# A transformer block's list schedule: another table of times for the prologue, and other keys, engines and a DMA allowance for the end

## The chip, the cores and the metric

The kernel runs on one core of a Trainium2 chip. The metric is the device time of one execution in microseconds. TensorE (PE) does the matmuls, VectorE (DVE), ScalarE (ACT) and GpSimd (POOL) the elementwise work; SyncE (SP) issues nearly all DMAs of this kernel, in the order in which they stand in its queue. Each engine takes its instructions in program order and waits for what an instruction needs, so what stands behind a waiting instruction waits too.

## The reference

One block with 2048 positions, D = 512, 32 heads of 16, a causal window of 256 and a hidden width of F = 1792, all in fp32:

```python
mod = (silu(c) @ w_mod).reshape(1, 6, 1, 512)          # sa, ca, ga, sb, cb, gb
h = layernorm(x) * (1 + ca) + sa
q, k, v = split(h @ wqkv)                              # 32 heads of 16
p = softmax(where(0 <= i - j < 256, q @ k.T / 4, -1e9))
x = x + ga * ((p @ v) @ wo)
h = layernorm(x) * (1 + cb) + sb
x = x + gb * ((silu(h @ w1) * (h @ w3)) @ w2)
```

## The kernel before

Each fp32 operand is split into a high part, which an ACT copy rounds, and a low part, the difference, which DVE or POOL computes; each product is three matmuls (high by high, high by low, low by high), 128x128 by 128x512 for the most part. The FFN's products are taken over two-by-two blocks of positions and of weights with seven products instead of eight.

The work falls into three stages, and every instruction's place is fixed by a program that sorts before anything is emitted:

1. *The prologue*, about the first 98 us. It loads x, makes the modulation of c, normalises (LN1), transposes, splits the result into hT and computes the values, and with them the first three `unit_a` (a head group's q and k for 512 positions) and the first two `unit_b` (scores for the row maxima). Every step is recorded as `at(t, fn)` with a time out of the tables `W` (for all but the units) and `Y` (for the units here), and the steps are emitted sorted by that time.
2. *The units*, to about 450 us: 32 rounds with the times of table `X`.
3. *The end*: wo with the gated residual, LN2, the FFN. `Sched.deal` is a list scheduler. Every operation has an engine, a cost, the operations it needs and a key; the scheduler goes through time and gives each engine the ready operation with the smallest key. The last units are in it as `fixed`. Table `K` holds the offsets of the keys, and in `by` and `be` the engines of the multiplications and low parts of the attention's output (`by`) and of the later splits of the FFN's inputs (`be`). `PEM` is an allowance added between ACT, DVE or POOL and a PE operation that uses their result; `QUIET` and `TW` are two more constants of this plan's time. The scheduler's times serve the order only: on the chip the order stays, and the times are what they are.

Tiles and lines of the profile that the text speaks of:

- *Prologue.* L410 and L412 fill ringq and ringk (the buffers of q and k for the scores) with their constant rows on POOL; L330 is the reciprocal root of LN1 (`rs0r`, `rs1r`) on POOL, L335 and L336 its statistics and L340 its application to `xt` on DVE; L631 transposes on PE, L347 applies the modulation on ACT and writes `h`, L349 and L350 split it into hT on DVE (L349 is the CAST, the high part). L653 and L438 are the matmuls of the values and of q and k; L423 and L427 split the weights of q and k. L572, L578, L583 and L592 make a gate's row of the modulation, L593 stores it to `g_dr`; it shares the buffer `h` with L347. L451 is the low part of q and k (`qk`), L457 and L459 are the DMAs that bring it into ringk and ringq, L537 loads x, L545 the modulation's weights, L419 those of q and k. L485 are the scores on PE, L494 their row maxima on DVE; L503 and L509 turn the maxima over (`mr`).
- *Last units.* L753 are the scores again, L773 a mask on DVE, L766 and L768 the exponentials on ACT, L721 the products with the values.
- *Attention's output.* L1072 takes the reciprocals of the sums of the softmax, which go to a buffer in memory (`r_dr`); L1104 multiplies the output (loaded from `o_dr`) with them; L1096 and L1099 split the result (`o`, or `x1b` for one block) into high and low part; L1116 are the matmuls with wo.
- *LN2.* L985, L990 and L993 add the residual and take the statistics, L1004, L1007 (the root, on POOL) and L1010 the row factors, L1236 applies them, L1250 transposes, L1254 modulates, L1267 forms sums and differences of blocks, L1273 and L1275 split them into `b`.
- *FFN.* L967 and L968 split weights, high part and low part. L1378 are the up products, L1401 to L1421 the combination of the seven and the gating up to L1405, L1449 the split of its result, L1471 the down products, L1476 adds them to x. L877 is work on the weights of later passes (`e`, `jb`) that fills gaps of POOL.

Of the kernel before, what the change touches and what calls it, by code (L numbers as in the profile page):

```python
# [39 lines left out]
         10.575, 10.975, 11.087, 6.249, 6.261), o=(11.83, 12.324), job=(0.275, 3.004, 9.681), gate=7.93)  # L40
Y = dict(wqk=(0, 4, 5), pj=(0.0, 0.382, 0.764, 1.146, 1.528, 1.91, 2.292, 2.674, 3.056, 3.438, 3.82, 4.202),
         ev=(4.614, 4.813), mix=(5.0,), row=(4.9, 4.9, 4.9, 5.1, 5.1, 5.1, 6.4, 6.4, 6.4), mx=(0.0, 0.5, 1.0, 1.5,
         2.0, 2.5, 3.0, 3.5, 4.0, 4.5, 5.0, 5.5, 6.0, 6.5, 7.0, 7.5), tl=(0.402, 0.402, 0.402, 0.402, 0.402,
         0.402, 0.402, 0.402, 0.402, 0.402, 0.402, 0.402, 0.402, 0.402, 0.402, 0.402), mr=(8.402, 8.563,
         8.761, 9.49))
MODE = 'CDCPCDCP'
W = dict(m=0.15, s=0.1, a=0.29, t=0.541, p=0.377, vs=1.762, vo=0.422, wq=(-1.8, 1.47, 1.5), wv0=-1.811, wvh=(-0.7, -0.65, -0.6, -0.55), wvl=(-0.5, -0.31, -0.3, -0.25), wp=1, A0=2.1, h0=0.539, h=6, hb=6.874, ls=3.287, la=1.146, rf=(1.55, 1.56, 8.4), v=2, vt=1.75, mr=(-1.85, 1.55), mm=(2.6, 4.625, 5.85, 7.075), ml=(-1.79, 1.25, 2.0, 4.9), A=1.268, At=7.876, B=9.889)
MXB = 3
# [64 lines left out]
class Sched:  # L113
# [36 lines left out]
    def deal(self):  # L150
# [5 lines left out]
        banks, fixed = list(self.banks), list(self.fixed)  # L156
        held = dict.fromkeys(CAPS, 0)
        given = dict.fromkeys(CAPS, 0)
        order, self.dealt = [], []

        def push(o):
            insort(ready[o.eng], (o.key, o.seq, o))
# [5 lines left out]
        while left:  # L168
            best = None
            for e, lst in ready.items():  # L170
                t, pick = free[e], None
                for key, seq, o in lst:
                    s = o.est
                    new = [b for b in o.bank if b.i is None]
                    if new:
# [6 lines left out]
                        s = max(s, at)  # L182
                    if o.kb:
# [3 lines left out]
                        s = max([s] + [u + 0.01 for u in self.urgent if b <= u < end])  # L187
# [7 lines left out]
            if fixed and (best is None or fixed[0][0] <= best[0]):  # L195

                t, e = max(free[fixed[0][2]], fixed[0][0]), fixed[0][2]
# [7 lines left out]
            elif fixed and (best is None or fixed[0][0] <= best[0]):  # L205
                t, fn, e, occ = fixed.pop(0)
# [5 lines left out]
            s, o = best  # L212
# [11 lines left out]
            if o.kb:  # L224
                s = max(s, lanes.pop(0))
# [19 lines left out]
            for u in o.users:  # L245
                m = PEM if u.eng == "PE" and o.eng in ("ACT", "DVE", "POOL") else 0.0
                u.est = max(u.est, s + (o.lat + m if u.eng != o.eng or o.kb else o.occ))
                u.need -= 1
                if not u.need:
                    push(u)  # L250
# [7 lines left out]

QUIET = 1.5
KEY = 1.715  # L260
# [3 lines left out]
def us(t):  # L264
# [3 lines left out]

TW = (231.0, 241.0, 0.8, 0.65)

# [5 lines left out]
NPE = 3  # L276

PEM = 0.8

BY = ((("POOL", "POOL"),) * 3 + (("DVE", "DVE"),), (("POOL", "POOL"),) * 3 + (("DVE", "DVE"),),  # L280
      (("POOL", "DVE"),) * 3 + (("DVE", "DVE"),), (("POOL", "POOL"),) * 4)
K = dict(be=(('DVE', 'DVE'), ('DVE', 'POOL'), ('DVE', 'POOL'), ('POOL', 'POOL'), ('POOL', 'DVE'),
         ('POOL', 'DVE'), ('DVE', 'DVE')), hr=0.109, de=7.098, wo=-0.159, x1=5.764, xb=-29.382,
         xl=0.241, os=-0.129, ol=(-15.316, -4.484, -6.572, 4.956), pl=(3.999, 1.87, -4.828,
         102.62), pe=(0.982, -5.962, 56.258, 232.622), o=(1.381, 8.497, 20.124, -0.531), n=(1, 1,
         2, 1), w0=62.113, l2=0.424, f=1.543, fl=40.897, by=((('POOL', 'POOL'), ('DVE', 'DVE'),
         ('DVE', 'POOL'), ('DVE', 'DVE')), (('DVE', 'DVE'), ('DVE', 'POOL'), ('DVE', 'DVE'),
         ('DVE', 'POOL')), (('POOL', 'POOL'), ('POOL', 'DVE'), ('DVE', 'POOL'), ('POOL', 'DVE')),
         (('POOL', 'DVE'), ('DVE', 'POOL'), ('DVE', 'POOL'), ('DVE', 'POOL'))), w=0.559, dn=1.412,
         ds=0.003, l3=-0.027)  # L290
@with_exitstack
# [1314 lines left out]
```

## Time and profile before

| | |
|---|---|
| time, median of 3 runs | 959.67 us (958.03 to 962.35) |
| profiled execution | 961.9 us |
| its span | 960.2 us |
| PE busy | 918.5 us, 96% |
| DVE, ACT, POOL busy | 672.0, 524.0, 541.5 us |
| mean granted clock of PE | 0.984 |

A row of the timeline reads: start in us, length in us, engine, line, operation, output and inputs, and in brackets the idle time of that engine in front of it and what ended it. `[2.23 <-DMA ringq<-qk]` on a PE row says that PE had nothing to do for 2.23 us until that DMA landed. A row with xN is N instructions in one. A busy row of DVE or POOL can itself be longer than usual when both work at once. PEclk is the clock that PE was granted, 1.00 being full.

### The profile page before, as it was taken

The page shows a single profiled execution, that of the slowest core. Times are in us where ns is not written, and L with a number is a line of the kernel's source. Part 1 is how long each engine was busy: PE and PEld are TensorE (multiplying, and loading weights), DVE is VectorE, ACT ScalarE, POOL GpSimd, SP SyncE. Part 2 cuts the span into 40 slices and gives each one's busy share as a digit, 9 for nine tenths or more (in the row PEclk, how much of TensorE's full clock was granted, in tenths as well). Part 3 has the DMA queues.
Part 4 walks back from the last instruction along what each step waited for, and adds up shares of the span by engine and source line. Part 5 has one row for each costly group of instructions (what it writes and reads, how often), then busy time and mean ns, then how long its engine had stood idle before and what let it go on. Part 6 is the DMA issues. An engine that isn't in the chain of part 4 may idle for free.

```text
span 960.2 us, 16729 instructions
## 1 busy us (share of the span) xinstructions
PE 918.5 (96%) x5330; PEld 710.2 (74%) x5330; DVE 672.0 (70%) x1864; ACT 524.0 (55%) x1031; POOL 541.5 (56%) x691
## 2 busy tenths in 40 slices
PE   5999999999999999988986989999999999999998
PEld 2678677777777777755664878888888888888886
DVE  7576689898988989886568465765559645565455
ACT  3333677787867777766577653333446334433330
POOL 5211565666666576645565688977647456443420
PEclk9999999999999999999998999999999999999999
DMA  9531365555655655466870577754335413312102
GB/s 306 171 93 46 93 181 162 158 158 151 191 154 151 159 157 158 135 181 195 250 232 1 184 243 277 235 188 162 98 122 191 167 58 99 99 61 85 36 23 88
DMA packets 125020, 141.62 MB, mean 147 GB/s; under 512 B 60034, under 2 KB 72834, under 8 KB 124932
## 3 DMA queue, kind: packets, MB, share of 16 engines
q1 hardware_dynamic: 124212, 139.51, 47.7%
q10 hardware_dynamic: 720, 1.05, 0.4%
q8 instruction: 42, 0.69, 0.3%
q14 instruction: 46, 0.38, 0.1%
HBM read 85.72 MB, written 34.61 MB: 125 GB/s over the span
## 4 chain that ended last, share of the span: by engine, by line
PE 76%; DVE 8%; DMA 4%; POOL 3%; ACT 3%; issue 3%; SPq 2%; POOLq 0%; DVEq 0%; ACTq 0%
PE mx L1378 10%; PE st L1378 10%; PE pj L438 9%; PE st L753 8%; PE po L721 8%; PE mx L485 7%; PE mx L1471 7%; PE st L1471 6%; PE st L653 4%; PE pj L1378 3%; PE pj L1471 2%; POOL w L968 1%; POOL e L877 1%; PE mx L1116 1%; PE mx L572 1%
## 5 line engine op out<-in xcount | busy, mean ns | idle before, releaser
L494 DVE CUSTOM_DVE_ANT_0 junk<-mx,mskq 128x320 bf16<-128x320 f32 (+4 forms) x512 | 223.3, 464 | 36.1 <-PE mx L485 34.9
L968 POOL TENSOR_TENSOR w<-w,w 128x512 fp32r<-128x512 f32 (+2 forms) x56 | 107.4, 1931 | 117.1 <-ACT w L967 71.2
L485 PE MATMUL mx<-ringk,ringq 96*128 96x320 f32 (+4 forms) x512 | 154.5, 324 | 5.3 <-DVE mt L494 3.0
L753 PE MATMUL st<-ringq,ringk 98*128 98x256 f32 (+1 forms) x528 | 140.9, 335 | 7.1 <-DVE st L773 3.3
L780 POOL TENSOR_SCALAR_AFFINE_SELECT pt<-pt 128x256 f32<-128x256 f32 x224 | 91.4, 408 | 80.8 <-ACT pt L768 73.2
L438 PE MATMUL pj<-hT,wq 128*128 128x512 f32 x384 | 133.2, 405 | 1.6 <-DVE wq L427 0.8
L485 PEld LDWEIGHTS mx<-ringk,ringq 96*128 96x128 f32 x512 | 98.0, 192 | 45.3 <-DVE mt L494 24.7
L768 ACT ACTIVATE pt<-st 128x512 f32<-128x512 f32 (+1 forms) x198 | 115.4, 587 | 25.0 <-DVE st L773 9.3
L753 PEld LDWEIGHTS st<-ringq,ringk 98*128 98x128 f32 x528 | 90.9, 192 | 22.3 <-ACT pt L768 5.9
L721 PE MATMUL po<-pt,vS 128*17 128x384 f32 (+2 forms) x1408 | 93.1, 395 | 0.3 <-ACT pt L768 0.3
L438 PEld LDWEIGHTS pj<-hT,wq 128*128 128x128 f32 x384 | 68.5, 192 | 10.1 <-DVE wq L427 1.2
L1378 PE MATMUL mx<-b,w 128*128 128x512 f32 x270 | 67.7, 396 | 6.0 <-ACT t L1412 5.7
L1409 DVE TENSOR_TENSOR t<-mx,t 128x512 f32<-128x512 f32 x49 | 33.7, 688 | 45.6 <-PE mx L1378 26.0
L1378 PEld LDWEIGHTS mx<-b,w 128*128 128x128 f32 x270 | 51.2, 191 | 17.3 <-ACT t L1412 6.0
L1409 DVE TENSOR_TENSOR t<-st,t 128x512 f32<-128x512 f32 x47 | 32.4, 689 | 44.0 <-PE st L1378 22.8
L773 DVE COPY_PREDICATED st<-later,st 128x256 f32<-128x256 uint8 x112 | 47.4, 424 | 22.5 <-PE st L753 19.2
L721 PEld LDWEIGHTS po<-pt,vS 128*17 128x17 f32 x1408 | 34.8, 98 | 36.9 <-issue 19.0
L1449 ACT ACTIVATE wq<-g 128x512 fp32r<-128x512 f32 x28 | 17.7, 631 | 80.7 <-DVE g L1405 33.2
L761 DVE TENSOR_TENSOR st<-st,mskr 128x256 f32<-128x256 f32 x125 | 53.6, 429 | 8.8 <-PE st L753 8.8
L795 POOL TENSOR_SCALAR_AFFINE_SELECT sm<-sm 128x256 f32<-128x256 f32 x109 | 42.4, 406 | 28.3 <-ACT sm L785 27.2
L1378 PE MATMUL st<-b,w 128*128 128x512 f32 x234 | 57.9, 390 | 0.0
L451 POOL TENSOR_TENSOR qk<-qkr,qk 128x512 fp32r<-128x512 f32 x32 | 42.1, 1316 | 25.5 <-ACT qk L447 25.5
(262 smaller groups left out, 2009.5 us busy)
## 6 DMA issues: line engine op xcount, KB each, us to landing
ringk<-qk SPq DMA_DIRECT2D x96, 128.0 KB
ringq<-qk SPq DMA_DIRECT2D x192, 64.0 KB
o_dr<-os SPq DMA_DIRECT2D x32, 256.0 KB
w<-wsum SPq DMA_DIRECT2D x14, 512.0 KB
w<-w2g SPq DMA_DIRECT2D x14, 512.0 KB
jb<-in_w SPq DMA_DIRECT2D x24, 256.0 KB
wraw<-in_w SPq DMA_DIRECT2D x7, 768.0 KB
w<-wraw SPq DMA_DIRECT2D x14, 384.0 KB
```

What stands on the lines that cost most here:

```text
L438: nc.tensor.matmul(v["ps"], WQ[g][w][:, n // 3], hTp(i, n // 3, b * BT, BT), start=(n == 0), stop=(n == 3 * KC - 1))
L485: nc.tensor.matmul(v[i][:, :n], both_queries(a, gs), keys(NS, a, (gs + 1) * HP - n, n), start=True, stop=True)
L494: nc.vector.tensor_tensor_reduce(out=junk[:, :n], in0=v[i][:, :n], in1=mskq[:, WK - n:], scale=1.0, scalar=-3e38, op0=ALU.add, op1=ALU.max ...
L721: nc.tensor.matmul(po[32 * i:32 * i + DH + 1, qb * P:(qb + nq) * P], vS[:, kb, 4 * g + i], pts[i // 2][:, i % 2, c0:c0 + nq], start=first, ...
L753: nc.tensor.matmul(o, keys(NM, a, kb * P, P), queries(a, q, n), start=q == lo, stop=not plus and q + n == hi, skip_group_check=True)
L761: nc.vector.tensor_tensor(out=ps, in0=ps, in1=mskk[:, p:p + 1].to_broadcast([P, 2, P]), op=ALU.add)
L768: nc.scalar.activation(held[u, j, a][:, :, :n], v[j, a, 0].rearrange("p (h q) k -> p h q k", h=2)[:, :, :n], AF.Exp, scale=SCALE)
L780: nc.gpsimd.affine_select(out=pt[:, :, 2 * m], in_=pt[:, :, 0], **w)
L968: sch.op(eng, lambda: on_eng(eng).tensor_tensor(out=lo(), in0=src(), in1=hi().bitcast(F32), op=ALU.subtract), 0.06 + 0.0024 * n if eng == ...
L1378: nc.tensor.matmul(ps(bk), WT[s, n][w][:, col], BB[t, k][r], start=start and c == 0, stop=stop and c == 5, skip_group_check=True)
L1409: return nc.vector.tensor_add(o, x, y)
L1471: nc.tensor.matmul(ps(bk), tiles[hk + (h,)][:, i * P:(i + 1) * P], w2_of(last, y, f), start=(m == 0), stop=(m == 5))
```

## The change

Only numbers change, and one allowance is new. `Y` and `W` get other values, so the prologue's steps are sorted otherwise; `K` gets other keys and, in `by` and `be`, other engines; `QUIET`, `TW[3]` and `PEM` move. The new `DM` = 0.076 is added in the plan to the landing of a DMA that carries data for an operation of an engine other than SP, if the DMA starts before the last operation of the units that are in the plan as `fixed`. `X`, the table of the units, stays, and so do the operations of the end and their needs.

```diff
-W = dict(m=0.15, s=0.1, ..., rf=(1.55, 1.56, 8.4), ..., mm=(2.6, 4.625, 5.85, 7.075), ml=(-1.79, 1.25, 2.0, 4.9), A=1.268, At=7.876, B=9.889)
+W = dict(m=0.18, s=0.307, ..., rf=(-1.1, -0.393, 6.445), ..., mm=(3.653, 5.841, 7.356, 7.655), ml=(-1.346, 1.651, 2.536, 6.904), A=1.465, At=7.897, B=10.563)
...
+        late = lambda o, u, s, stop=fixed[-1][0]: o.kb and u.eng != "SP" and s < stop
...
             for u in o.users:
-                m = PEM if u.eng == "PE" and o.eng in ("ACT", "DVE", "POOL") else 0.0
+                m = PEM if u.eng == "PE" and o.eng in ("ACT", "DVE", "POOL") else DM if late(o, u, s) else 0.0
                 u.est = max(u.est, s + (o.lat + m if u.eng != o.eng or o.kb else o.occ))
...
-QUIET = 1.5
+QUIET = 1.487
...
-TW = (231.0, 241.0, 0.8, 0.65)
+TW = (231.0, 241.0, 0.8, 0.583)
...
-PEM = 0.8
+PEM = 0.998
+DM = 0.076
...
-K = dict(be=(('DVE', 'DVE'), ('DVE', 'POOL'), ('DVE', 'POOL'), ('POOL', 'POOL'), ('POOL', 'DVE'),
-         ('POOL', 'DVE'), ('DVE', 'DVE')), hr=0.109, de=7.098, wo=-0.159, x1=5.764, xb=-29.382,
+K = dict(be=(('POOL', 'DVE'), ('POOL', 'DVE'), ('DVE', 'POOL'), ('POOL', 'POOL'), ('POOL', 'POOL'),
+         ('POOL', 'POOL'), ('DVE', 'POOL')), hr=2.855, de=12.48, wo=-3.567, x1=16.6, xb=-38.041, xl=-26.167,
...
```

*The prologue, SP's queue ahead of the first scores.* `g_dr` is a gate's row, `ringk` and `ringq` the buffers of the scores, `xt` a tile of x, the `qk` tiles the high parts and (the last ringk and ringq here) the low part of the first unit. Before:

```order
L537 DMA xt<-in_x 128x512 x2
L593 DMA g_dr<-h_413 1x512
L457 DMA ringk<-qk_432 32x2x512
L459 DMA ringq<-qk_432 16x16x64 x2
L457 DMA ringk<-qk_432 32x2x512
L459 DMA ringq<-qk_432 16x16x64 x2
L593 DMA g_dr<-h_470 1x512
L537 DMA xt<-in_x 128x512 x2
L457 DMA ringk<-qk_452 32x2x512
L459 DMA ringq<-qk_452 16x16x64 x2
```

Now:

```order
L459 DMA ringq<-qk_432 16x16x64 x2
L457 DMA ringk<-qk_432 32x2x512
L459 DMA ringq<-qk_432 16x16x64 x2
L419 DMA wqr<-in_wqk 128x512
L537 DMA xt<-in_x 128x512 x2
L593 DMA g_dr<-h_486 1x512
L457 DMA ringk<-qk_432 32x2x512
L593 DMA g_dr<-h_498 1x512
L457 DMA ringk<-qk_453 32x2x512
L459 DMA ringq<-qk_453 16x16x64 x2
```

The two loads of x between the last gate row and the first unit's last rows now stand ahead of both gate rows, and so does the load of weights that followed.

*The prologue, POOL.* Before:

```order
L330 TENSOR_TENSOR rs1r<-rs1v,nhalf 128x4
L451 TENSOR_TENSOR qk_452<-qkr,qk_432 128x512
L665 MEMSET vS 128x384
L410 MEMSET ringq 98x1024 x2
L412 MEMSET ringk 2x2x512
```

Now:

```order
L330 TENSOR_TENSOR rs1r<-rs1v,nhalf 128x4
L410 MEMSET ringq 98x1024 x2
L412 MEMSET ringk 2x2x512
L451 TENSOR_TENSOR qk_453<-qkr,qk_432 128x512
L665 MEMSET vS 128x384
```

The last fills of the rings moved from behind the low part of the first unit to right behind the root of LN1's second block. On PE the first score now stands behind 66 matmuls of the values and 16 of q and k; it stood behind 55 and 14.

*The units' end, DVE.* L773 is the mask that PE waits for, L1104 and L1072 belong to the attention's output. Before:

```order
L773 COPY_PREDICATED st<-later,st 128x2x128
L1104 TENSOR_TENSOR wq_7426<-wq_7426,wq_7445 128x512
L1104 TENSOR_TENSOR qkr<-qkr,qk_7464 128x512
L1072 RECIPROCAL mT<-mT 32x128
L773 COPY_PREDICATED st<-later,st 128x2x128
L1099 TENSOR_TENSOR x1b<-qkr,x1b 128x512
L773 COPY_PREDICATED st<-later,st 128x2x128 x2
```

Now:

```order
L773 COPY_PREDICATED st<-later,st 128x2x128
L1104 TENSOR_TENSOR qk_7400<-qk_7400,qk_7413 128x512
L773 COPY_PREDICATED st<-later,st 128x2x128
L1104 TENSOR_TENSOR wq_7426<-wq_7426,wq_7447 128x512
L1072 RECIPROCAL mT<-mT 32x128
L1104 TENSOR_TENSOR qkr<-qkr,qk_7525 128x512
L773 COPY_PREDICATED st<-later,st 128x2x128 x2
```

One mask moved ahead of the multiplications and the reciprocal; the last two stand behind the multiplication of `qkr`, as before.

*The FFN's start, ACT.* L1412 copies the first product out of its bank (`mx` or `st`), L1273 are the high parts of `b`, L1096 those of the attention's last block. Before:

```order
L1254 ACTIVATE t_8172<-st,modc 128x512
L1273 ACTIVATE b_7816<-t_8157 128x512
L1273 ACTIVATE b_7800<-t_8172 128x512
L1096 ACTIVATE o_7150<-wq_8026 128x512
L1096 ACTIVATE o_7150<-qk_7899 128x512
L1273 ACTIVATE b_7808<-t_8149 128x512
L1273 ACTIVATE b_7812<-t_8187 128x512
L1412 ACTIVATE t_8196<-mx 128x512
```

Now:

```order
L1254 ACTIVATE t_8185<-mx,modc 128x512
L1273 ACTIVATE b_7789<-t_8168 128x512
L1273 ACTIVATE b_7781<-t_8160 128x512
L1273 ACTIVATE b_7773<-t_8185 128x512
L993 ACTIVATE st,sqB_8045<-x1b,nmB_8044 128x512
L1273 ACTIVATE b_7785<-t_8201 128x512
L1412 ACTIVATE t_8208<-st 128x512
L1096 ACTIVATE o_7150<-wq_7930 128x512
```

Two of the high parts of the attention's last block went elsewhere, and the copy reads another kind of bank. On PE, 12 matmuls of L1116 that stood behind the first two up products now stand ahead of them, and both products are in banks named `st`, which the first two had not used. Elsewhere, on POOL: ahead of LN2's first root, between the first and the second low part of a weight (L968), stand one L1104 and two L1099, where one L1099 stood; and ahead of the L1421 that the first down products' gating waits for stand five L877 behind the L968 in front, where eight stood.

25 lines of the change are left out of this document (12 added, 13 removed).

## The prediction

> **What bounds the kernel now.** I read the page's busy times first, then the clock in windows, then the waits of PE alone, and then the timeline around each long wait. From the page, busy us, share of the span and instructions:
>
> ```profile
> PE 918.5 (96%) x5330; PEld 710.2 (74%) x5330; DVE 672.0 (70%) x1864; ACT 524.0 (55%) x1031; POOL 541.5 (56%) x691
> ```
>
> TensorE is the bound, and the change adds and removes no matmul. Time can come only from two things: PE's idle places, and stretches at half clock. The second view is busy time by window (us, then each engine, then the granted clock as PEclk):
>
> ```profile
> 46.33:49.74 3.41, 1.18 (x6) 0.71 (x5) 3.27 (x9) 0.00 (x0) 0.00 (x0) 1.00 0.79 251
> 49.74:53.15 3.41, 3.41 (x9) 2.65 (x9) 0.63 (x6) 0.13 (x1) 1.01 (x1) 0.50 0.48 172
> 452.52:455.93 3.41, 2.21 (x11) 1.28 (x10) 2.71 (x5) 2.58 (x5) 0.51 (x2) 1.00 0.93 276
> 455.93:459.34 3.41, 3.41 (x27) 1.34 (x28) 0.17 (x1) 0.87 (x2) 2.72 (x5) 0.50 0.99 277
> 575.39:578.80 3.41, 3.41 (x10) 2.63 (x9) 1.70 (x3) 1.24 (x2) 3.25 (x5) 0.50 0.93 356
> 600.00:700.00 100.00, 100.00 (x443) 82.82 (x442) 61.60 (x81) 37.45 (x58) 75.44 (x71) 1.00 0.50 164
> ```
>
> From 600 to 700 PE never idles: 443 matmuls in 100 us, 0.226 us each. Each half-clock window is 3.41 us long, and the two whose forerunner is shown stand right behind a window in which PE idled 1.2 and 2.2 us (3.41 less 2.21 and 1.18); at clock 0.50 it loses half its work, 1.7 us. So an idle place can cost its length and 1.7 us more. The third view is what PE waited for (us in total, times, longest):
>
> ```profile
> PE mx L1378 <- ACT t L1412: 5.7, 1, 5.7
> PE st L753 <- DVE st L773: 3.3, 3, 2.0
> ...
> PE st L1471 <- DVE x1a L1476: 2.3, 1, 2.3
> PE mx L1250 <- ACT wqr L1236: 2.2, 1, 2.2
> PE mx L1116 <- DVE o L1099: 1.7, 1, 1.7
> PE mx L509 <- DVE mr L503: 1.2, 3, 0.5
> PE pj L438 <- DVE wq L427: 0.8, 1, 0.8
> ...
> PE pj L438 <- ACT wq L423: 0.7, 1, 0.7
> ```
>
> These are one-time waits at seams between stages. The largest of each stage is what the new order can touch; part of L773's 3.3 us lies where both orders are alike, and stays. The rows further down add two of the same kind, for ringq (2.2) and for L494 (0.9).
>
> **The change, place by place.** Nothing computed changes; each cost below is a wait that goes, comes or moves.
>
> *Prologue, the first scores.* The 2.2 us wait for ringq, before half clock at 49.74. The timeline shows the chain (start, us, engine, line):
>
> ```profile
> 3.71 1.84 POOL L410 MEMSET ringq<- 98x1024 f32 x2
> ...
> 3.80 1.90 DVE L404 CAST mskr<-wqr 128x256 fp32r<-128x256 f32 x1 [2.34 <-POOL wqr L398]
> ...
> 27.89 0.55 DVE L340 TENSOR_SCALAR xt<-xt,mv,rs1r 128x512 f32<-128x512 f32 x1 [1.20 <-POOL rs1r L330]
> ...
> 34.71 0.60 PE L631 MATMUL st<-ident,xt 128*128 128x128 f32 x4
> ...
> 39.45 3.45 DVE L349 CAST hT<-h 128x512 fp32r<-128x512 f32 x1 [0.46 <-ACT h L347]
> ...
> 40.71 1.91 POOL L410 MEMSET ringq<- 98x1024 f32 x2
> ...
> 43.72 0.59 ACT L592 ACTIVATE h<-mx 1x512 f32<-1x512 f32 x1 [2.43 <-DVE hT L350]
> ...
> 44.67 0.84 SPq L537 DMA_DIRECT2D xt<-in_x  x2
> ...
> 49.44 0.27 PE L485 MATMUL mx<-ringk,ringq 96*128 96x64 f32 x1 [2.23 <-DMA ringq<-qk]
> ```
>
> All casts of hT together (min, median and max in ns):
>
> ```profile
> L349 DVE CAST hT<-h x16: 423/428/3447, 17.9 to 84.1; 128x512 fp32r<-128x512 f32 x16
> ```
>
> The one beside POOL's ring fills took 3.45 us, eight times the median. L592 waited for it 2.43 us, and SP's queue (gate row, two x loads, ringk, ringq) waited for L592. In the new order the fills leave this place, and the x loads go ahead of the gate rows. The chain from L592's start to the first scores was 5.7 us (49.44 less 43.72); without the 0.84 us of x loads it is 4.9. Between the last L583 and the first scores PE now has 20 values and 4 products: 24 x 0.226 = 5.4 us. So the wait goes, 0.5 us to spare: -2.2, and the half clock behind it -1.7. Together -3.9 (bounds -1.6, a landing 0.6 us late with the clock still cut, and -3.9).
>
> Where do the fills go? Right behind POOL's rs1r (L330), which is also what releases L340 at 27.89. L404 above shows the price: a DVE operation that starts just behind two fills runs 1.9 us, until they end. L340's four would then be done some 1.4 to 2.9 us later (two fills, or with L412 as well); the transposes L631 that use them stood at 34.71 and come at about 32.6 (1.3 us less of PE's work ahead by the new order, 0.8 less of waits below), while four L340 of 0.55 would be done at 30.1, so 2.5 us are slack. I take +0.6 (0 to +2.9, if the casts behind slip too).
>
> By the Trainium skill's GPSIMD Engine Reference, section 1 Specifications, GpSimd shares its SBUF interfaces with VectorE and contends with its two-port and two-input instructions. The two casts agree; by that rule the fills' price moves to L340 rather than vanishing, and the sum would be about 2 us worse.
>
> Two small waits: the first weights' L423 and L427 come a step earlier against PE, 0.8 of their 1.5 us (0 to -1.5), and L494 no longer stands behind a row of statistics before the score at 71.76:
>
> ```profile
> 71.76 0.41 PE L485 MATMUL mx<-ringk,ringq 96*128 96x320 f32 x1 [0.91 <-DVE mt L494]
> ```
>
> -0.9 (0 to -0.9). These three: -1.1 (+2.9 to -2.4).
>
> *Units' end.* DVE runs in order. The mask L773 stood behind L1104, which waits for a DMA, and behind L1072:
>
> ```profile
> 453.21 0.69 DVE L1104 TENSOR_TENSOR qkr<-qkr,qk 128x512 f32<-128x512 f32 x1 [1.33 <-DMA r_dr<-wqr]
> ...
> 455.13 0.50 PE L753 MATMUL st<-ringq,ringk 98*128 98x512 f32 x1 [0.98 <-DVE st L773]
> ```
>
> In the new order that L773 stands ahead of both; the last two L773 stand behind the DMA wait, and PE asks for them later than it ends. -1.2 of idling (3.41 less 2.21) and half of the 1.7 us at 455.93, since the same clock window keeps some idling: -2.0 (0 to -2.9).
>
> *LN2's start.* PE's 2.2 us wait for L1236, whose chain runs through POOL's queue to the root L1007:
>
> ```profile
> 477.01 0.85 ACT L967 ACTIVATE w<-w 128x768 fp32r<-128x768 f32 x1 [4.22 <-DMA w<-wraw]
> ...
> 479.74 1.75 POOL L1099 TENSOR_TENSOR o<-wq,o 128x512 fp32r<-128x512 f32 x1
> ...
> 483.82 1.01 POOL L1007 TENSOR_TENSOR rsB<-sqB,nhalf 128x4 f32<-128x4 f32 x1
> ...
> 486.58 1.26 POOL L1104 TENSOR_TENSOR wq<-wq,wq 128x512 f32<-128x512 f32 x1
> ```
>
> This gets worse. The first L968 of POOL's queue waits for L967, and so for the landing of the weight. Between it and the next L968, ahead of the root, POOL now has one L1104 and two L1099; before there was one L1099. One more of each, 1.3 and 1.7 us, is +3.0. PE has six more matmuls of L1116 ahead of the turns, -1.4. +1.5 (bounds -1.0, if the weights land earlier with the shorter seam before, and +3.5, with half clock).
>
> *FFN's start.* The largest: 5.7 us for L1412 and 1.7 for L1099.
>
> ```profile
> 514.41 3.42 DVE L1267 TENSOR_TENSOR t<-t,t 128x512 f32<-128x512 f32 x2
> ...
> 518.40 0.58 ACT L1412 ACTIVATE t<-mx 128x512 f32<-128x512 f32 x1
> ```
>
> L1412 frees the bank that the second product needs, and sits in ACT's queue behind cuts L1273 that wait for DVE's L1267 (1.7 us each here). In the new order the count of L1267 and L1275 ahead of the last cut that the second product needs is about the same, so PE gets past this place no earlier than 519; but it has done 12 more matmuls of L1116 and three more of L1378 by then, 15 x 0.226 = 3.4 us. The lo part that made PE wait 1.7 moves from DVE to POOL, ahead of the L1267. A wait of about 4.4 us stays, so I count nothing for the clock. -3.4 (-0.5, if L1267 begins 3 us later, to -5.9 with one half-clock window less).
>
> *First down products.*
>
> ```profile
> 565.68 4.11 POOL L877 TENSOR_TENSOR e<-e 128x128 f32<-128x128 f32 x8
> ...
> 569.75 1.29 POOL L1421 TENSOR_TENSOR t<-t,t 128x512 f32<-128x512 f32 x1
> ...
> 571.07 2.83 DVE L1405 TENSOR_TENSOR g<-t,g 128x512 f32<-128x512 f32 x1 [2.64 <-POOL t L1421]
> ```
>
> PE's 2.3 us for L1476 goes back over L1405 to L1421, behind eight L877 of 0.51 us. Three go elsewhere: L1421 comes 1.5 us earlier and 0.8 us of the wait stays. -1.5, and half of the half clock at 575.39: -2.3 (0 to -3.9).
>
> *Half turn and the rest.* Ten instead of six of the splits of b go to POOL, and one L1421 is later; PE is covered by its own queue there (not one idle row in 600 to 700): 0 (0 to +2).
>
> Sum: -3.9 - 1.1 - 2.0 + 1.5 - 3.4 - 2.3 + 0 = -11.2. The profiled execution took 961.9 us (span 960.2 and 1.7 around it): 950.7. It is 2.2 us above the median of 959.67, about one half-clock window and a bit, which a median run has not to give back; I therefore subtract less from the median, 9.7, and forecast 950.
>
> **A rule against it.** The Trainium skill's TensorE: Matmul & The Clock Gate, section "HAM oscillation", gives the rule that only gaps of PE over some 3.4 us cut the clock. The rows differ: windows with 1.2 and 2.2 us of idling are followed by 0.50. By the rule the half-clock windows at 49.74, 455.93 and 575.39 would have another cause and stay. That is the first rival.
>
> **Rivals.**
> - *The half clock stays or moves* (the cut falls on another seam, since waits as long stay, for L773, L1236 and L1412): the 1.7, 0.8 and 0.8 us drop out, 950 + 3.4 = 953.4. For it: the windows at 49.74, 455.93 and 575.39 lie 119 and 35 times 3.413 us apart, on one grid, so a shift of everything behind 50 us gives each remaining wait another phase. Against: removing waits removes causes.
> - *POOL's queue at LN2 carries through.* The root at +3.5 and, because the cuts of b follow from it, FFN's start gives nothing: 950 + 2.0 + 3.4 = 955.4.
> - *The waits only move*: each seam's next latest thing is as late; prologue alone gives 2 us. About 958. Against it: the first scores' margin is counted in matmuls.
> - *Slower: units out of step.* Units follow each other without slack for L503 (the waits for mr, 0.4 us each, in 3 of 32). If the prologue hands over its third unit_a or second unit_b late, each unit could wait about 0.5, the longest seen: 30 x 0.5 = 15, and 965. It decides from 0.5 us a unit on. Against it: the units' own order is word for word the same, and in the profile the waits do not recur every unit.
>
> **How the numbers follow.** A measurement of this kernel can tell about 0.5%, 4.8 us, from no change (its runs lie between 958.03 and 962.35). Forecast 0.52, 944 to 953; half clock stays 0.18; POOL's queue 0.12; waits only move 0.09; slower 0.09. Faster by over 0.5% (below 954.9) is the first two: 0.70; within 0.5% the next two: 0.21; slower 0.09. With all unknown costs at their good ends the sum is near -20 (940), at their bad ends near +5 (965); 942 to 961 leaves out the slower case and about 0.1 at the lower end.
>
> **What would show it.** Right: the first score has no DMA wait, clock 1.00 around 50 us and no CAST of hT far over its 0.43; L753 no wait for L773 after 450; the L1378 wait at about 4.4; the L1476 wait under 1. Wrong: L340 of 1.5 us and more with transposes L631 waiting; the wait for L1236 over 5 us; new waits for L509 in each unit.

## The result: 951.1 us, 0.990 of the time before

The changed kernel takes 951.11 us (median of 4 runs, 947.54 to 952.83), the kernel before 959.66 us on the same chip (median of 4). The ratio is 0.9904, with a 95% interval of 0.9877 to 0.9931: faster by about 1%, against a forecast of 950 us. On another chip, in a later series (e9 below), the ratio was 0.9888 (0.9868 to 0.9907). The profiled execution of the changed kernel took 952.1 us, its span 950.3.

The page's busy times and the list of PE's waits (us in total, times, longest), after:

```profile
PE 916.3 (96%) x5330; PEld 710.3 (75%) x5330; DVE 670.0 (71%) x1861; ACT 525.1 (55%) x1031; POOL 545.6 (57%) x694
```

```profile
...
PE mx L1250 <- ACT wqr L1236: 3.0, 1, 3.0
PE mx L1116 <- ACT t L1254: 2.7, 1, 2.7
PE st L753 <- DVE st L773: 2.5, 3, 2.1
...
PE st L753 <- ACT pt L768: 2.1, 2, 1.8
...
PE pj L1116 <- POOL o L1099: 1.5, 1, 1.5
PE st L1378 <- ACT t L1412: 1.3, 1, 1.3
...
PE st L1471 <- ACT e L1315: 0.5, 1, 0.5
```

The same 5330 matmuls. The wait of 5.7 us for L1412 is now 1.3, with a new one of 2.7 for L1254 in front of it; the 1.7 for L1099 on DVE is now 1.5 for L1099 on POOL; the DMA wait of the first score and the 2.3 for L1476 are gone; the wait for L1236 grew from 2.2 to 3.0.

To see where the time came from, the span is cut at the same events in both traces: PE's first matmul, the first score L485, the 33rd L485 (the units' start), then the 401st L485, the last L721, the first and the last L1250, the 31st L1378 and the 61st L1471. The windows view of PE alone (from:to, length, busy, matmuls, granted clock, then DMA share and GB/s), before and after:

```profile
8.51:49.44 40.93, 36.89 (x185) 1.00 0.71 237
49.44:100.92 51.48, 50.55 (x241) 0.97 0.22 60
360.86:468.45 107.59, 100.14 (x767) 0.95 0.60 172
468.45:487.54 19.09, 16.86 (x81) 1.00 0.95 283
487.54:503.25 15.71, 14.58 (x71) 0.89 0.68 218
503.25:536.11 32.86, 25.03 (x101) 0.90 0.12 36
536.11:604.87 68.76, 66.32 (x296) 0.98 0.74 250
```

```profile
8.52:49.31 40.79, 39.60 (x198) 0.96 0.74 245
49.31:95.05 45.74, 45.74 (x228) 1.00 0.22 59
356.38:460.83 104.45, 98.60 (x762) 0.93 0.60 170
460.83:483.36 22.53, 19.55 (x96) 1.00 0.97 297
483.36:499.26 15.90, 15.20 (x67) 0.79 0.51 182
499.26:528.01 28.75, 23.35 (x98) 0.94 0.11 35
528.01:594.84 66.83, 65.25 (x295) 1.00 0.75 254
```

Some of the work lies in another of these stages now. The same view for the products with wo alone (L1116) has 21, 72, 39 and 60 of them in the third to the sixth row of the first list, and 15, 84, 36 and 57 in the second. The two rows of the stage ahead of LN2's first turn, before and after:

```profile
468.45:487.54 19.09, 16.66 (x72) 1.00 0.95 283
```

```profile
460.83:483.36 22.53, 19.35 (x84) 1.00 0.97 297
```

A matmul that has moved costs 0.226 us here and gives it back there. With that taken out (six products fewer, twelve more, three fewer, three fewer), the stages stand beside the prediction's terms as follows:

| stage | length, after less before | moved L1116 | left | the prediction |
|---|---|---|---|---|
| to the units' start | -0.14 and -5.74 | | -5.9 | -3.9 - 1.1 = -5.0 |
| units up to the 401st L485 | 261.33 - 259.94 = +1.39 | | +1.4 | 0 |
| units' end | -3.14 | -1.36 | -1.8 | -2.0 |
| LN2, to the first turn and to the last | +3.44 and +0.19 | +2.71 and -0.68 | +1.6 | +1.5 |
| FFN's start | -4.11 | -0.68 | -3.4 | -3.4 |
| up products, first down products | -1.93 | | -1.9 | -2.3 |
| the rest | 350.97 - 351.25 = -0.28 | | -0.3 | 0 |

The sum is -10.3 us between the last matmuls of the two traces, against -11.2. PE's busy time for the same 5330 matmuls fell by 2.2 us of it (918.5 to 916.3), which is what the clock gave; the other 8.1 us are idle time. The prediction's terms have 3.4 us for the clock and 7.8 for waits.

### The profile page after: what moved, and what is told of

It reads as the page before. It is cut to its first block, busy times and chain, and to the rows that moved or that the text cites. A ratio compares the mean times of both kernels' runs of the same rounds, so it can differ in the third digit from the quotient of the medians.

```text
span 950.3 us, 16719 instructions
## 1 busy us (share of the span) xinstructions
PE 916.3 (96%) x5330; PEld 710.3 (75%) x5330; DVE 670.0 (71%) x1861; ACT 525.1 (55%) x1031; POOL 545.6 (57%) x694
## 4 chain that ended last, share of the span: by engine, by line
PE 78%; DVE 6%; DMA 4%; POOL 4%; ACT 3%; issue 2%; SPq 2%; POOLq 0%; DVEq 0%; ACTq 0%
PE st L1378 11%; PE mx L1378 10%; PE pj L438 8%; PE st L753 8%; PE mx L485 8%; PE po L721 8%; PE st L1471 7%; PE mx L1471 7%; PE st L653 5%; PE pj L1378 3%; PE pj L1471 2%; DMA r_dr<-mT 1%; DVE t L1267 1%; DVE b L1275 1%; DMA qk<-o_dr 1%
## 5 line engine op out<-in xcount | busy, mean ns | idle before, releaser
L494 DVE CUSTOM_DVE_ANT_0 junk<-mx,mskq 128x320 bf16<-128x320 f32 (+4 forms) x512 | 223.4, 464 | 39.6 <-PE mx L485 39.0
L968 POOL TENSOR_TENSOR w<-w,w 128x512 fp32r<-128x512 f32 (+2 forms) x56 | 107.0, 1924 | 111.6 <-ACT w L967 61.8
L485 PE MATMUL mx<-ringk,ringq 96*128 96x320 f32 (+4 forms) x512 | 154.9, 326 | 2.2 <-DVE mt L494 2.2
L485 PEld LDWEIGHTS mx<-ringk,ringq 96*128 96x128 f32 x512 | 98.6, 193 | 41.4 <-DVE mt L494 23.1
L768 ACT ACTIVATE pt<-st 128x512 f32<-128x512 f32 (+1 forms) x198 | 115.2, 587 | 24.7 <-DVE st L773 10.5
L721 PE MATMUL po<-pt,vS 128*17 128x384 f32 (+2 forms) x1408 | 92.7, 394 | 0.0
L1378 PE MATMUL st<-b,w 128*128 128x512 f32 x270 | 67.8, 391 | 1.3 <-ACT t L1412 1.3
L721 PEld LDWEIGHTS po<-pt,vS 128*17 128x17 f32 x1408 | 34.6, 98 | 36.3 <-issue 19.8
L1378 PE MATMUL mx<-b,w 128*128 128x512 f32 x240 | 59.9, 389 | 0.0
L773 DVE COPY_PREDICATED st<-later,st 128x256 f32<-128x256 uint8 x112 | 47.5, 424 | 17.3 <-PE st L753 12.7
L1378 PEld LDWEIGHTS st<-b,w 128*128 128x128 f32 x270 | 50.5, 188 | 12.1 <-ACT t L1412 1.7
L967 ACT ACTIVATE w<-w 128x512 fp32r<-128x512 f32 (+2 forms) x56 | 42.5, 786 | 20.7 <-DMA w<-wsum 11.2
```

Of the source, the lines that this page charges most:

```text
L485: nc.tensor.matmul(v[i][:, :n], both_queries(a, gs), keys(NS, a, (gs + 1) * HP - n, n), start=True, stop=True)
L494: nc.vector.tensor_tensor_reduce(out=junk[:, :n], in0=v[i][:, :n], in1=mskq[:, WK - n:], scale=1.0, scalar=-3e38, op0=ALU.add, op1=ALU.max ...
L721: nc.tensor.matmul(po[32 * i:32 * i + DH + 1, qb * P:(qb + nq) * P], vS[:, kb, 4 * g + i], pts[i // 2][:, i % 2, c0:c0 + nq], start=first, ...
L768: nc.scalar.activation(held[u, j, a][:, :, :n], v[j, a, 0].rearrange("p (h q) k -> p h q k", h=2)[:, :, :n], AF.Exp, scale=SCALE)
L968: sch.op(eng, lambda: on_eng(eng).tensor_tensor(out=lo(), in0=src(), in1=hi().bitcast(F32), op=ALU.subtract), 0.06 + 0.0024 * n if eng == ...
L1378: nc.tensor.matmul(ps(bk), WT[s, n][w][:, col], BB[t, k][r], start=start and c == 0, stop=stop and c == 5, skip_group_check=True)
```

## The experiments

In all diffs below, "..." stands for numbers or lines left out. Times are medians; a ratio is to the kernel before on the same chip. e1 to e4 ran on one chip, e5 to e8 on a second and e9 to e12 on a third, so kernels are best compared within these three groups.

### e1 and e2: the two halves alone

e1 is the kernel before with the new `Y` and `W`, e2 the kernel before with everything else.

```diff
-Y = dict(wqk=(0, 4, 5), pj=(0.0, 0.382, ...
-W = dict(m=0.15, s=0.1, ...
+Y = dict(wqk=(-1.668, 4.008, 4.272), pj=(0.205, 0.587, ...
+W = dict(m=0.18, s=0.307, ...
```

> The kernel before with only the new tables Y and W of the prologue; the end keeps its old keys and engines. Theory A (each place pays for its own wait): PE reaches the first scores of the units some 5.9 us earlier, as in the changed kernel, and keeps about 4.5 of it behind the half-clock windows, so 955.2 us, ratio 0.995. Theory B (what the waits cost is set by where they fall on the 3.41 us grid of the clock, so parts do not add up): the first 5.9 us are there, but what arrives at the end differs from 4.5 by a window or two, 951 to 958. Rival C (the prologue's gain is lost in the units, which run in step with something else): 959.

```diff
-QUIET = 1.5
+QUIET = 1.487
+DM = 0.076
...
-K = dict(be=(('DVE', 'DVE'), ...
+K = dict(be=(('POOL', 'DVE'), ...
```

> The kernel before with only the new keys K, engines, QUIET, TW, PEM and DM of the end; the prologue keeps its old tables. Theory A: the end's own share, 10.3 less 4.5, so about 5.8 us, 953.9 us, ratio 0.994. Theory B: the half-clock windows behind the waits of L773 and L494 near 420 and 437, which are double in the changed kernel and single before, stay single, so 2 to 3 us more than A: 951. Rival C (the end gains only because the prologue shifted it): 958 or more.

e1: 956.13 us, ratio 0.9969 (0.9952 to 0.9987). e2: 952.86 us, ratio 0.9936 (0.9915 to 0.9957). The product of the two is 0.9905, that of the whole change, on another chip, 0.9904: the halves add up, as theory A has it (e1 by itself 0.002 short of its 0.995), and two thirds of the gain are the end's. The intervals are some 2 us wide to either side, though, so the one window by which theory B would have the parts differ is not excluded.

e2 shows something else. Its prologue is that of the kernel before, and its first score waited too, but for 1.39 us and with no half clock behind it. Timeline of e2, and its windows on the 3.41 us grid of its own half-clock windows:

```profile
48.89 0.27 PE L485 MATMUL mx<-ringk,ringq 96*128 96x64 f32 x1 [1.39 <-DMA ringq<-qk]
```

```profile
44.45:47.87 3.42, 3.05 (x14) 1.00 0.80 224
47.87:51.28 3.41, 2.39 (x12) 1.00 0.75 240
```

The wait from 47.50 to 48.89 lay across a border of the grid, 0.37 us in one window and 1.02 in the next, and neither was followed by half clock. In the profile of before one window held 2.23 us of it.

### e3: the rings' fills put back

```diff
-W = dict(..., rf=(-1.1, -0.393, 6.445), ...
+W = dict(..., rf=(-1.1, -0.393, 8.4), ...
```

> The changed kernel with one number of W set back: the last ring fills go behind the low part of the first unit again, beside the casts of hT; SP's queue keeps the new order. Theory A as the prediction has it (the cast held by the fills, 1.9 us of the chain, and the x loads, 0.84 us, both had to go): the fills run from about 39.7 to 43.5 us, a cast of hT takes 2 to 3.4 us again, L592 or L347 comes 1.5 to 2 us later, the first score waits 1 to 1.5 us and a half-clock window may follow: 0.5 to 3 us slower than the changed kernel, 952 to 954; and L340 runs at 0.55 instead of 1.03. Rival (the x loads ahead of the gate rows are what mattered, the cast has slack now): no wait for the first score, 951, same as the changed kernel.

951.82 us, ratio 0.993 (0.9906 to 0.9954), which overlaps the changed kernel's. Its timeline, and below it that of after, show what the fills' place changes:

```profile
28.61 1.92 DVE L340 TENSOR_SCALAR xt<-xt,mv,rs1r 128x512 f32<-128x512 f32 x4 [1.06 <-POOL rs1r L330]
...
43.30 0.93 DVE L349 CAST hT<-h 128x512 fp32r<-128x512 f32 x1 [3.62 <-ACT h L347]
...
49.14 0.20 PE L485 MATMUL mx<-ringk,ringq 96*128 96x64 f32 x1
```

```profile
28.54 1.85 POOL L410 MEMSET ringq<- 98x1024 f32 x2
28.63 4.12 DVE L340 TENSOR_SCALAR xt<-xt,mv,rs1r 128x512 f32<-128x512 f32 x4 [1.07 <-POOL rs1r L330]
...
32.38 0.75 PE L631 MATMUL st<-ident,xt 128*128 128x128 f32 x4
...
49.31 0.20 PE L485 MATMUL mx<-ringk,ringq 96*128 96x64 f32 x1
```

Beside the fills four L340 took 4.12 us instead of 1.92, and the transposes were not held up. With the fills back in their old place a cast of hT took 0.93 us, and the first score waited for nothing either. In the traces the fills' move is worth nothing to PE, on either side; the two ratios, taken on different chips, would leave room for some 2 us.

### e4: PE kept busy through two waits

Twelve repeats of one score product ahead of the wait at 417 us and fourteen of another ahead of the one at 434; each writes the same values again.

```diff
-            nc.tensor.matmul(v[i][:, :n], both_queries(a, gs), ...)
+            for _ in range(13 if COUNT[0] == 491 else 1):
+                nc.tensor.matmul(v[i][:, :n], both_queries(a, gs), ...)
...
+                for _ in range(15 if COUNT[1] == 497 else 1):
+                    nc.tensor.matmul(o, keys(NM, a, kb * P, P), queries(a, q, n), ...)
```

> The changed kernel with 12 more of one score matmul in front of PE's wait for L773 near 417 us, and 14 more of one in front of its wait for L494 near 434 us: PE repeats the same product into the same bank while it would idle. Nothing else changes. Theory A on the clock (a wait of 2 us within a window, not the page's 3.4, is what cuts the clock for the two windows behind it): the windows at 418 to 425 and 435 to 442 run at 1.00, which lost 2.7 and 3.0 us of work there: 5 us faster than the changed kernel, about 946. By the page's rule the idle time of 2 us has nothing to do with the clock: the windows stay at 0.50, the time stays 951 or rises a little. Rival: the repeated matmuls delay the results that DVE and ACT wait for, and the waits grow by what was filled: 951 to 955.

947.41 us, ratio 0.988 (0.9858 to 0.9903). Four windows of after, and the second and fourth of them in e4:

```profile
414.94:418.35 3.41, 2.21 (x16) 1.00 0.47 115
418.35:425.18 6.83, 5.40 (x22) 0.50 0.83 240
432.01:435.42 3.41, 2.28 (x13) 1.00 0.70 192
435.42:442.25 6.83, 6.01 (x33) 0.50 0.62 195
```

```profile
418.35:425.18 6.83, 6.40 (x49) 1.00 0.89 269
...
435.42:442.25 6.83, 6.47 (x51) 1.00 0.58 173
```

Where PE is given useless work in place of waiting, the half clock behind is gone in this execution: 49 matmuls instead of 22 in the first pair's 6.83 us, 51 instead of 33 in the second's. From 405 to 461 us its trace gains 1.9 us on the changed kernel's, not the 6.8 that four half windows at 1.7 each would give, since PE then waits longer for the exponentials (L768, 3.6 us in its list of waits, 2.1 before). In the medians the gain over the changed kernel is within the error of the ratios.

### e5: LN2's root first

One exchange in POOL's row, made after the plan:

```diff
+    p = place(("root", 0))
+    push_back(max(i for i in range(p) if seq[i][0] == "POOL"), 1)
```

> The changed kernel, with one pair exchanged on POOL: LN2's first root (L1007, rsB <- sqB) is put ahead of the 1024 wide L968 that held it for 2.3 us (477.83 to 480.19 in the profile of after). Theory A (the loss of the changed kernel at LN2's first turn is the root's place in POOL's row, and nothing else holds the turn): PE's wait <- ACT wqr L1236 falls from 3.0 to about 0.6 us and the time by 2.4, to 948.7 us, ratio to the kernel before 0.988; up to 1.7 us more if the half clock behind the wait goes too. Rival B (the time is taken back within LN2, because the products that follow wait for the L968 that is now later, or for the o tiles): the wait at the first turn falls as in A, another one of about 2 us shows by 510 us, and the ratio stays at 0.990. Rival C (squares of the weights are due sooner than I think): slower by over 1 us.

951.56 us, ratio 0.9928 (0.9912 to 0.9943): no gain. The timeline of after, and then of e5 (where lines stand 4 or 6 further down: L1011 is L1007, L1014 is L1010, L1242 is L1236):

```profile
477.83 2.39 POOL L968 TENSOR_TENSOR w<-w,w 128x1024 fp32r<-128x1024 f32 x1
480.19 1.01 POOL L1007 TENSOR_TENSOR rsB<-sqB,nhalf 128x4 f32<-128x4 f32 x1
481.24 1.22 DVE L1010 TENSOR_TENSOR nbB<-nmB,rsB 128x4 f32<-128x4 f32 x1 [1.76 <-POOL rsB L1007]
482.50 0.81 ACT L1236 ACTIVATE wqr<-x1a,nbB,rsB 128x512 f32<-128x512 f32 x1 [1.25 <-DVE nbB L1010]
```

```profile
478.51 1.02 POOL L1011 TENSOR_TENSOR rsB<-sqB,nhalf 128x4 f32<-128x4 f32 x1
479.50 3.60 POOL L972 TENSOR_TENSOR w<-w,w 128x1024 fp32r<-128x1024 f32 x2
479.93 1.97 DVE L1014 TENSOR_TENSOR nbB<-nmB,rsB 128x4 f32<-128x4 f32 x1
481.94 0.81 ACT L1242 ACTIVATE wqr<-x1a,nbB,rsB 128x512 f32<-128x512 f32 x1 [0.15 <-DVE nbB L1014]
```

The root came 1.7 us earlier. But the four-column multiplication after it, beside the L968 that now runs at that moment, took 1.97 us instead of 1.22, and its consumer came only 0.6 us earlier. This execution had been 0.6 us behind the other at the units' end, so from there to the first turn it gained 1.2 us; PE's wait fell from 3.0 to 1.8, half of what theory A expected. POOL's row was a part of the price at LN2 and not all of it. One execution is not much for this, since the wait for L1236 differs between executions of one order; but in the eight profiles that have the changed kernel's order of POOL's row here (after, e2, e3, e4, e6, e7, e9, e10) it is 2.0 to 3.1 us, and in the four with the root first (e5, e8, e11, e12) 0.8 to 1.8. At the end the trace of e5 is 0.5 us ahead, less than the scatter of the runs.

### e6: the table load ahead of the units

```diff
+    at(h0 + W["B"] + W["At"] + Y["mr"][1] + 0.05, lambda: nc.scalar.activation(sc, sc, AF.Exp))
```

> The changed kernel, with one Exp on a small tile that nobody reads put ahead of the units on ACT, so that the 1.28 us table load at 95.93 us (L768 ACT_TABLE_LOAD) lies earlier. Theory A (the load stands in the units' first chain, and PE's 1.77 us wait at 95.6 us is made of it): that wait falls below 0.6 us, the doubled half-clock window at 97.5 us goes or shrinks, and the time falls by 1.3 to 4.5 us: 947 to 950, ratio 0.986 to 0.989. Rival B (the units wait for the maxima of L494 and not for ACT): the wait stays, and the ratio is 0.990.

947.94 us, ratio 0.9899 (0.988 to 0.9918). The median is 3.6 us below that of e5 beside it, but the ratio is no lower than the changed kernel's (0.9904, and 0.9888 in e9). Timeline of after, then of e6:

```profile
95.93 1.28 ACT L768 ACT_TABLE_LOAD   x1
...
97.88 0.58 PE L753 MATMUL st<-ringq,ringk 98*128 98x256 f32 x1 [1.77 <-ACT pt L768]
```

```profile
96.44 0.38 PE L754 MATMUL st<-ringq,ringk 98*128 98x256 f32 x1 [0.34 <-ACT pt L769]
...
215.37 0.39 PE L754 MATMUL st<-ringq,ringk 98*128 98x256 f32 x1 [0.96 <-ACT pt L767]
```

The load was the wait, as theory A had it: 1.77 us became 0.34, and no half clock followed. At 215 us this trace is 3.6 us ahead of the changed kernel's. Then comes the last row, a wait that the changed kernel does not have there; at 221 us the lead is 2.4 us, and at 349 us 2.3. What the load itself is worth shows beside e10 below.

### e7: two reciprocals later

```diff
+    push_back(place(("recip", 0, 0)), 6)
+    push_back(place(("recip", 0, 6)), 6)
```

> The changed kernel, with two reciprocals L1072 (at 418.45 and 434.89 us, each idle 1.74 us on DVE for a DMA) put behind six more of DVE's instructions; nothing else is moved. Theory A (these two waits of DVE are PE's waits of 2.06 and 1.95 us at 417 and 434 us, and the cause of the two doubled half-clock windows): both waits fall below 0.7 us, the windows at 418 and 435 us go, and the time falls by 4 us for the waits and up to 6 for the clock, less what ACT and POOL then are late by: 943 to 948 us, ratio 0.982 to 0.988. Rival B (what e4 showed: with the clock kept, the probabilities and tiles of the units are the next bound, and only half of it is left): 948 to 949 us, ratio 0.988 to 0.989. Rival C (the products that need the reciprocals, r_dr and L1104, become the late ones): a new wait of PE at L1116 and 951 us or more.

948.77 us, ratio 0.9902 (0.9885 to 0.9919). The waits of 2.06 and 1.95 us became 1.12 (for L494) and 1.42 (for L768), and the half clock moved behind those: 3.4 us at 422.3 and 6.8 at 429.1. At the last L721 its trace is 0.9 us ahead of the changed kernel's. By the ratio there is no gain over the changed kernel. That is rival B's mechanism, with less than it gave: the exponentials on ACT (4.3 us of waits in all, 2.1 before) are next in line.

### e8: the three together

> The changed kernel with the three edits of this call together: root L1007 ahead of the 1024 wide L968, the Exp table loaded before the units, two reciprocals L1072 six DVE instructions later. Theory A (three places, each with PE as the one that waits, so that the gains add up): 951.1 less 2.4, 1.3 and 4 us is 943.4 us, ratio 0.983; with the half-clock windows gone down to 939. Rival B (the later places take back what the earlier ones gain): no faster than the best of the three alone, ratio 0.987 or more.

945.78 us, ratio 0.9864 (0.9845 to 0.9883), between the two theories' values and 2.2 us below the best of the three alone. The first turn's wait fell to 0.8 us, further than with the root alone.

### e9: the changed kernel again

> The changed kernel itself, unaltered, as the reference for the three others on the same chip. All theories: a ratio to the kernel before of 0.990 (0.988 to 0.993). In its profile the half-clock windows may lie in other places than in the first profile of it; theory A (the windows' grid starts at another phase in every execution, and a wait of about 2 us is cut or not by where it falls) expects the same waits at 95.6, 417 and 434 us to within 0.1 us, and windows that differ in place or length; the rival (the windows belong to the waits) expects the same windows.

950.22 us, ratio 0.9888. The waits were those of the first profile (1.76, 2.05 and 1.99 us, ending at 97.98, 419.78 and 436.82, and 3.1 at LN2); the windows were not. The half clock behind the first was 3.4 us at 99.42 instead of 6.8 at 97.50, and behind the third 3.4 instead of 6.8. Up to the last matmul it had seven 3.41 us windows of half clock, against ten. This is theory A.

### e10: the old unit table

```diff
-Y = dict(wqk=(-1.668, 4.008, 4.272), pj=(0.205, 0.587, ...
+Y = dict(wqk=(0, 4, 5), pj=(0.0, 0.382, ...
```

> The changed kernel with the unit's table Y of the kernel before; the table in front of the units (W) and the end stay new. Theory A (what moved the units' start by 5.9 us is mainly the row of PE that Y gives, with 13 more products ahead of the first score): the first score waits 1 us or more again, the units start 2 to 5 us later than in the changed kernel, and the time is 953 to 956 us, ratio 0.993 to 0.996. Rival B (W alone carries it, by its loads of x and its casts): the units start within 1 us of the changed kernel's 95.05 us, and the ratio is 0.990.

950.36 us, ratio 0.9882 (0.9862 to 0.9903), the same as e9 beside it. The units start at 95.16 us and the first score stands at 49.45 with no wait, behind as many matmuls as in the changed kernel. `W` carries the prologue's gain, and `Y` nothing that can be measured. It also had the wait of 1.77 us at the units' start, with no half clock behind it. Its windows, on its own grid:

```profile
93.29:96.70 3.41, 2.67 (x12) 1.00 0.28 82
96.70:100.11 3.41, 2.13 (x11) 1.00 0.51 122
```

A border of the grid at 96.70 cut this wait in two, and with a wait of 0.25 us just in front of it the two windows hold 0.74 and 1.28 us of idle time. In the first profile of after the border came later, at 97.50, and one window holds 1.64 us:

```profile
94.09:97.50 3.41, 1.77 (x8) 1.00 0.34 105
97.50:104.33 6.83, 6.45 (x23) 0.50 0.55 124
```

By 217 us e10's trace is 2.6 us ahead of that one, and no other difference between the two is seen. So of e6's 3.6 us about 1.0 was the load, and the rest a window that another execution doesn't have anyway. Nor did the 1.0 last: the L721 that starts at 348.55 us in after starts at 346.30 in e6 and at 345.92 in e10, where the load is in its old place. The load was that wait, but that moving it shortens the kernel is not shown.

### e11 and e12: versions that beat both

e11 is e8 with repeats ahead of its next waits; e12 is the changed kernel with e4, e5 and e6 in one.

```diff
+EXTRA = {482: 5, 487: 5, 501: 11}
...
+                for _ in range(1 + EXTRA.get(COUNT[0], 0)):
+                    nc.tensor.matmul(o, keys(NM, a, kb * P, P), queries(a, q, n), ...)
```

> The kernel of e8, with 21 score products (L753) repeated at three places ahead of its waits at 416.7, 424.8 and 434.0 us (5, 5 and 11 repeats, about 1.1 us each), so that PE is busy where it stood still. Theory A (short waits still cut the clock there: e8 has half clock at 417.5 for 6.8 us and at 438.0 for 3.4 us): both windows go, the waits shrink to below 0.3 us, and the time is 2 to 4 us below that of e8, ratio 0.982 to 0.985. Rival B (the stretch is bound by ACT, POOL and the DMAs, and PE waits by as much more when its clock is whole): ratio 0.986 as e8, with new waits of about 2 us between 417 and 445.

> The changed kernel with the Exp table loaded before the units, LN2's root ahead of the 1024 wide L968, and the 26 repeats of e4 ahead of the waits at 417 and 434 us; the reciprocals stay where they are. Theory A (the gains of e4 (2.3 us), e6 (2 to 3.8) and e5 (0.5 to 1.2) lie in different places and add up): 944 to 946 us, ratio 0.982 to 0.985, faster than e8 or the same. Rival B (what the units gain ahead of 400 us is lost at the waits for the DMAs at 417 and 434, which come by the SP queue's time): 947 us, ratio 0.988 as e4.

e11: 946.35 us (943.93 to 946.85), ratio 0.9845 (0.9824 to 0.9865), 3.9 us below e9 on the same chip, with no run in common. It is the fastest by ratio; e8, on another chip, lies within its interval. The half clock at 417.5 and 438.0 went, as theory A said, and a wait of 2.0 us for L768 at 423.6 came, with half clock behind it, as rival B said. e12: 947.57 us, ratio 0.9861 (0.9835 to 0.9888), between its theories too. Its interval overlaps that of e9, so of the two only e11 is clearly faster than the changed kernel.

## Why the prediction was right

The sum missed by 0.9 us of 11, and its waits held: 8.1 us of idle time went, where the terms had 7.8. The clock gave 2.2 us instead of 3.4. Most terms held by their own mechanism; at LN2 and at the FFN's start the sizes agree better than the mechanism does, and that is luck.

*First scores, -3.9, and the rest of the prologue, -1.1: measured -5.9 together.* The wait of 2.2 us went because PE had 13 more products to do ahead of the first score, which starts when it did (49.31 against 49.44 us); they are 2.9 us of work. The shorter chain of SP's queue, the other reason I gave, is not needed beside them, and no run has it alone. In the two stages PE's idle time fell from 4.97 to 1.19 us, by 3.8 where I had 3.3, and its busy time for the same 426 matmuls from 87.44 to 85.34, by 2.1 where I had 1.7. Two parts of the step were off. The cast of 3.45 us, from which the chain started, is not a property of that order: in e2, the same prologue, the longest cast there took 0.95 us, and the wait was 1.39. And the price of +0.6 for the fills' new place was zero: L340 did run 2.2 us longer in all, as the Trainium skill's GPSIMD Engine Reference, section 1 Specifications, lets one expect of a shared interface, but the 2.5 us of slack that I had counted covered it. The row of my working that gave the slack was right, and the term I took did not follow it. Which numbers of `W` put the 13 products forward was not tried; `Y` (e10) and the fills (e3) are excluded.

*Half clock behind the first score, 1.7 of the 3.9.* It went, though not by merit of this change alone: e2 has the old order and no window there. All windows lie on a grid of 3.41 us, whose phase differs from execution to execution, and whether half clock follows a wait goes with how the grid's border divides it (e2, e10). Over all 14 profiles, from PE's first matmul on, each full-clock window of this grid with over 1.75 us of PE idle was followed by half clock; of those with 0.8 to 1.75 some were (1.64 us in after, at 94.09) and some were not (1.73 in e1, at 500.63). Idle time is not the whole rule: in after, e5, e6 and e7 a half-clock window near 16 us stands behind one with only 0.1 to 0.5 us of idle time. Why is open.

That is the first rival's mechanism, and in part it came. The three windows that the forecast took away (49.74, 455.93 and 575.39) are gone, and the two of the FFN's start are one; but four that were single before are double after (at 97.50, 418.35, 435.42 and 483.21), and one at 15.58 is new, so the profiled executions had nine and ten. The +1.4 us in the units goes with the doubled window at 97.5, where before had a single one. The Trainium skill's TensorE: Matmul & The Clock Gate, section "HAM oscillation", speaks of gaps over some 3.4 us. e4 contradicts it here: two waits of 2.0 us, filled, took their windows with them.

*Units' end, -2.0: -1.8.* Of it 1.6 us are idle time and 0.2 the clock, where I had 1.2 and 0.8. Behind 450 us one wait for L773 is left, of 0.15 us, as forecast.

*FFN's start, -3.4: -3.4,* but by another sum. I expected 4.4 us of waiting to stay, all of it for L1412. PE idled 5.4 us: 2.7 for L1254, 1.3 for L1412, and 1.5 for L1099, a wait that I had counted as gone with that operation's move to POOL. Before it was 7.8, so the waits gave 2.4, and the other 1.0 is the clock, for which I had counted nothing. The chain was the right one: the L1254 stands in ACT's row behind an L1273 that waits for DVE's L1267, as L1412 did before.

*First down products, -2.3 and half turn, 0: -1.9.* The wait for L1476 went whole, and one of 0.5 us for L1315 came in its place, where I had 0.8 left. Three small waits at L1378 (0.6, 0.2 and 0.2 us) are new, so the idle time fell by 0.9 instead of 1.5; the clock gave 0.8, as forecast, and one product lies in another stage. These three gains of the end are read from the traces, and e2 has them only together; no run takes one alone.

*LN2's start, +1.5: +1.6*, with 0.75 of it in the wait for L1236 and the rest in the turns, which ran at a mean clock of 0.79 instead of 0.89. The raw difference at the first turn, 3.4 us, looks like twice the term; the twelve moved products are the other 2.7. POOL's row did nearly what I had summed up: counted from the last L721 the root came at 19.4 us instead of 15.4, and six products that moved behind that L721 are 1.4 of these 4.0, which leaves 2.6 against +3.0. But the wait grew by 0.75 only, where 3.0 less 1.4 gives 1.6, in part because L1010 behind the root took 1.22 us instead of 1.77; the half clock in the turns, which I had only in the bound, made up for it. Rival two, in which this delay carries through to the FFN, is refuted by the -3.4 that follows, and so is the one in which the units fall out of step: L503's waits in the list are 0.5 us in all.

*From the profile to the forecast.* I took 1.5 us less from the median than from the profiled execution, since that one was slow by about a clock window. The profiled executions differ by 9.8 us, the medians by 8.6.

## What to carry to other kernels

Before a stage is called slower or faster, count the matmuls in it on both sides: a moved product shows as a loss in one stage and a gain in the next, and it is neither. Short one-time waits at the seams came back here nearly in full, 8.1 us for the 7.8 that were counted, but half clock behind them differs between executions of one kernel (ten windows in after, seven in e9), and a single profile cannot price it; look at a second one. When a wait is taken away, name what stands next in line: the waits for L768, the exponentials on ACT, took back 1.5 us of the 4.0 that e4 filled and 2.2 of the 4.0 that e7 went for.

## What the runs showed of the hardware

- *The clock's windows.* Half clock comes in windows of 3.41 us or two of them, on a grid that is fixed within an execution. An idle time of 1.64 us inside one window was followed by half clock (after, 94.09); where a border split the same wait, so that the windows held 0.74 and 1.28 us, none followed (e10).
- *Small operations of DVE beside POOL.* A 128x4 multiplication (L1010) took 1.97 us in e5, 1.22 in after, and in before 1.77, next to an L968:

```profile
484.81 1.80 POOL L968 TENSOR_TENSOR w<-w,w 128x768 fp32r<-128x768 f32 x1
484.86 1.77 DVE L1010 TENSOR_TENSOR nbB<-nmB,rsB 128x4 f32<-128x4 f32 x1 [1.95 <-POOL rsB L1007]
```

Both end within 0.02 us of each other, at 486.61 and 486.63. The Trainium skill's SBUF — State Buffer, section "SBUF: two separate sides", says that whichever of a two-input DVE operation and a GpSimd operation starts first holds the shared pair to its end. These rows agree.
- *Loading the Exp table* took ACT 1.28 us at its first use, in the middle of the chain that the units start with; in e6 one use on a small tile put it ahead of the units.
